# Seven block products in place of eight for a third of the tokens, with weight sums on GpSimd

## The chip, the cores and the metric

The kernel runs on one core of a Trainium2 chip. The metric is the device time of one execution in microseconds (us); the median of three runs is compared. Inputs and outputs lie in the chip's HBM. In the profile PE is TensorE's matmuls, PEld its weight loads, DVE is VectorE, ACT is ScalarE, POOL is GpSimd and SP is SyncE, whose queue issues most of the transfers.

## The reference

An attention block with a decay per head is followed by a mixer over tokens and channels.

```python
# q, k, v: (4, 8, 768, 64); blocks of 64 tokens, decay lam per head
intra = (q_b k_b^T * Dmask) v_b ;  inter = (q_b * lam_pow) kv_state
out_b = intra + inter ;  kv_state = lam**64 * kv_state + (k_b * rev_pow)^T v_b
x = out as (4, 768, 512)
xt = x.transpose(0, 2, 1)
h = xt @ U @ V                                   # U (768, 32), V (32, 768)
u = x + h.transpose(0, 2, 1)
ch = np.maximum(u @ w_ch1, 0.0) @ w_ch2          # (512, 2048), (2048, 512)
return (u + ch).astype(np.float32)
```

U, V, w_ch1 and w_ch2 come as float64, so each weight is read as two 32-bit words per element and converted on the chip. The two products with w_ch1 and w_ch2, over 3072 tokens, are the largest part of the work.

## The kernel before, in words

The 3072 tokens are six groups `g` of `N` = 512. The 2048 hidden columns are 16 tiles `ft` of 128. To keep float32 accuracy with TensorE's faster float32 type, each operand is split into a high part, a low part and a third part that mixes the two. A product of two blocks is then three matmuls, two adding to a bank `pz` and one to a bank `pd`; the value is `4097 * pz + 4096 * pd` with the scales used here.

The stages are, in the order of time:

- *Attention and mixer* (to about 114 us): an order written out by hand (`pieces`). Its output `u` is stored (`store`, `u_d`), turned by TensorE (`turn`) and split (`L609`, `L610`, `L613`, or `L640`, `L641`, `L633`) into `uhl` and `ud`, which stay in SBUF for all six groups.
- *First product* (114 to about 383 us): `hidden(ft, pair)` does one unit, a tile `ft` for a pair of groups: 16 matmuls to `pz` (L837), then 8 to `pd` (L848). ScalarE reads `pz` out (L844), VectorE adds `pd` (L853), and the result goes to HBM as `r_d[ft][g]` (L854). The first six units (`head`) are ordered by hand among the last pieces of the mixer. Then 33 units run tile by tile (`body`, `ft` 2 to 12) and 9 pair by pair (`tail`, `ft` 13 to 15). From the body on, a scheduler sets each engine's order. `banks` gives two sets of PSUM banks in turn.
- Beside these units `run_units` hands out the steps that make the weights. `weight_steps` fetches the float64 words (L146) and builds float32 from them: shifts and masks on VectorE (L166, L155), two exponent steps on ScalarE (L173, L174), three more steps on VectorE (L184, L192, L197). `split_steps` splits the result (L215, L220, L227, for w2 also L224). A tile of w1 goes into `w1_pool` (3 buffers) for `hidden`; a split tile of w2 goes to HBM (`w2_d`, 768 KB each) and comes back later (`w2_back`).
- *Second product* (to the end): 96 steps (`steps`, six groups by 16 tiles). `fetch` brings `r_d` back, `split` makes relu and the three parts (L952 on ScalarE; L953 and L954 on VectorE), `product` does 12 matmuls of 512 columns (L969, L971, L973). `ahead` runs the fetch three steps and the split two steps ahead. After 16 steps `finish` reads out four tiles (L990, L994) and adds `u` on GpSimd (L998).

Of the kernel before, what the change touches and what calls it, by code (L numbers as in the profile page):

```python
# [14 lines left out]
P = 128  # L15
# [3 lines left out]
def kernel(  # L19
# [61 lines left out]
    mix_ctx = ctx.enter_context(ExitStack())  # L81
    att_ctx = ctx.enter_context(ExitStack())
# [19 lines left out]
    w2_d = [dram.tile([P, 3, C], FP32, name=f"w2_d{ft}") for ft in range(FT)]  # L102
# [100 lines left out]
    def split_steps(tile_of, src, in_parts=False, scale=None, apart=False):  # L203

        st = {}

        def dst():
            if "w" not in st:
                st["w"] = wconv.tile([P, C], FP32, tag="wf", name="wf")
            return st["w"]  # L210

        def five():
            st["o"] = o = tile_of()
            st["t"] = o[:, 0, :].bitcast(FP32)
            on_scalar(lambda: nc.scalar.mul(o[:, 0, :], st["w"], NEAR))  # L215

        def six():
            w, low = st["w"], st["o"][:, 1, :]
            st["low"] = low.bitcast(FP32) if scale is None else w
            nc.vector.tensor_tensor(  # L220
                out=low if scale is None else w, in0=w, in1=st["t"], op=ALU.subtract
            )
            if scale is not None:
                on_scalar(lambda: nc.scalar.mul(low, w, scale))  # L224

        def seven():
            nc.vector.scalar_tensor_tensor(  # L227
                st["o"][:, 2, :], st["t"], -E, st["low"], ALU.mult, ALU.add
            )

        return weight_steps(dst, src, C, in_parts=in_parts, apart=apart) + [five, six, seven]

    w1v, w2v = {}, {}

    def w1_steps(ft, in_parts=False, apart=False):
        def tile_of():
            w1v[ft] = w1_pool.tile([P, 3, C], F32R, tag="w1", name="w1")
            return w1v[ft]

        cols = moe_w_ch1[:, ft * P : (ft + 1) * P].rearrange("(c p) f -> p c f", p=P)  # L240
        return split_steps(tile_of, cols, in_parts, apart=apart)
# [340 lines left out]
    def columns(what, g, ct):  # L582
        return what[:, ct, :] if g >= FG else by_halves(what)[:, :, ct, :]

    def like(out, g):
        return out if g >= FG else out.rearrange("p (t i) -> p t i", i=D)

    hl_at, d_at = [hl_pool], [d_pool]
# [4 lines left out]
    def turn(s):  # L593

        g, n = divmod(s, TG)
        if n == 0:
            uhl[g] = hl_at[g >= FG].tile([P, 2, CT, N], F32R, tag="hl", name="u_hl")
            ud[g] = d_at[g >= FG].tile([P, CT, N], F32R, tag="d", name="u_d")
        if g >= FG:
            cols = slice(n * P, (n + 1) * P)  # L600
            hi, low, diff = uhl[g][:, 0, :, cols], uhl[g][:, 1, :, cols], ud[g][:, :, cols]
            pt = bank([P, CT, P], "put", "b1")
            for ct in range(CT):
# [5 lines left out]
            nc.scalar.mul(hi, pt, E * NEAR)  # L609
            nc.vector.scalar_tensor_tensor(  # L610
                low, hi.bitcast(FP32), -1.0 / E, pt, ALU.mult, ALU.add
            )
            nc.gpsimd.tensor_tensor(  # L613
                out=diff, in0=hi.bitcast(FP32), in1=low.bitcast(FP32), op=ALU.subtract
            )
# [188 lines left out]
    def enter_first_product(s):  # L804
# [3 lines left out]
        for pools, name in ((hl_at, "hl_b"), (d_at, "d_b")):  # L808
            pools.append(
                ctx.enter_context(tc.tile_pool(name=name, bufs=NG - FG, reuse_waits="tile"))  # L810
            )
# [11 lines left out]
    def hidden(ft, pair, before={}):  # L823
# [28 lines left out]
        for g in pair:  # L852
            nc.vector.scalar_tensor_tensor(rs[g], acc[g][1], 4096.0, rs[g], ALU.mult, ALU.add)  # L853
            nc.sync.dma_start(out=r_d[ft][g], in_=rs[g])  # L854
# [218 lines left out]
```

## Time and profile before

| what | value |
|---|---|
| runs | 648.42, 649.17, 649.84 us; median 649.17 us |
| span of the profiled execution, first to last instruction | 648.1 us |
| PE busy | 639.3 us, 99% of the span |
| PEld, DVE, ACT, POOL busy | 539.3, 434.7, 268.8, 116.3 us |
| granted TensorE clock | 1.00 |
| moved by DMA | 131.69 MB, mean 203 GB/s |

The profiled execution's own time is not recorded apart from its span; the span is 0.3 us under the fastest run and 1.1 us under the median. Matmuls are pipelined, so their mean in the profile (389 to 391 ns for 512 columns) is longer than the time from one to the next. Durations of POOL are rough.

### The profile page before, as it was taken

The numbers are of one execution on the slowest core, as the hardware profiler recorded it, in microseconds if no ns is written. First come the engines' busy times: TensorE is split into PE (matmuls) and PEld (weight loads), VectorE is DVE, ScalarE is ACT, GpSimd is POOL, SyncE is SP. The second block draws the span as 40 slices with busy tenths as digits, with TensorE's granted clock in tenths as the row PEclk, the third lists the DMA queues.
The fourth block names the chain that finished last, engine by engine and source line by source line (L and its number), as shares of the span: only waits on it lengthen the run. The fifth ranks groups of instructions, "written<-read, shape, count | busy, mean of one in ns | idle before, by whom it ended". The sixth has DMA issues, their size and how long they took to land.

```text
span 648.1 us, 13405 instructions
## 1 busy us (share of the span) xinstructions
PE 639.3 (99%) x5242; PEld 539.3 (83%) x5242; DVE 434.7 (67%) x709; ACT 268.8 (41%) x500; POOL 116.3 (18%) x104
## 2 busy tenths in 40 slices
PE   9899999999999999999999999999999999999997
PEld 8888989788888888888888888888888888888886
DVE  6656878668997777777796244685575665755854
ACT  3675766435755444444454222332322322322320
POOL 4475968330000000000000000030030300300300
PEclk9999999999999999999999999999999999999999
DMA  9979996354876555655587899864363363543521
GB/s 232 241 182 272 231 242 163 119 191 176 287 258 219 209 207 209 207 209 211 211 292 276 320 332 392 287 220 138 96 227 98 123 204 97 172 152 99 179 82 65
DMA packets 132737, 131.69 MB, mean 203 GB/s; under 512 B 81538, under 2 KB 90754, under 8 KB 132674
## 3 DMA queue, kind: packets, MB, share of 16 engines
q1 hardware_dynamic: 107552, 124.41, 59.1%
q10 hardware_dynamic: 25122, 6.42, 4.4%
q8 instruction: 41, 0.67, 0.4%
q14 instruction: 22, 0.18, 0.1%
HBM read 80.09 MB, written 50.33 MB: 201 GB/s over the span
## 4 chain that ended last, share of the span: by engine, by line
PE 97%; ACT 1%; issue 1%; DMA 1%; DVE 0%; ACTq 0%; DVEq 0%
PE pz L837 27%; PE pd L848 13%; PE pz L971 13%; PE pz L969 13%; PE pd L973 13%; PE px L459 4%; PE pss L408 4%; PE px L470 2%; PE pqk L361 2%; PE pkv L431 1%; PE pm L563 1%; PE pp L486 1%; PE pm L626 1%; DMA kraw<-in_k_dram 1%; PE put L604 1%
## 5 line engine op out<-in xcount | busy, mean ns | idle before, releaser
L837 PE MATMUL pz<-u_hl,w 128*128 128x512 f32 x768 | 185.0, 391 | 0.0
L837 PEld LDWEIGHTS pz<-u_hl,w 128*128 128x128 f32 x768 | 143.7, 188 | 30.2 <-ACT r L844 0.6
L971 PE MATMUL pz<-w_hl,m 128*128 128x512 f32 x384 | 148.7, 389 | 0.0
L969 PE MATMUL pz<-w_hl,m 128*128 128x512 f32 x384 | 148.3, 389 | 0.0
L973 PE MATMUL pd<-w_d,m 128*128 128x512 f32 x384 | 147.4, 389 | 0.0
L952 ACT ACTIVATE m<-rm 128x512 fp32r<-128x512 f32 x96 | 60.6, 632 | 182.3 <-PE pd L973 125.5
L953 DVE SCALAR_TENSOR_TENSOR m<-rm,m 128x512 fp32r<-128x512 f32 x96 | 71.6, 748 | 95.7 <-ACT m L952 95.7
L998 POOL TENSOR_TENSOR o<-o,u 128x512 f32<-128x512 f32 x20 | 29.8, 1523 | 433.1 <-DVE o L994 433.1
L853 DVE SCALAR_TENSOR_TENSOR r<-pd,r 128x512 f32<-128x512 f32 x96 | 61.7, 685 | 60.4 <-ACT r L844 48.2
L848 PE MATMUL pd<-u_d,w 128*128 128x512 f32 x384 | 95.7, 390 | 0.0
L971 PEld LDWEIGHTS pz<-w_hl,m 128*128 128x128 f32 x384 | 72.1, 188 | 15.0
L969 PEld LDWEIGHTS pz<-w_hl,m 128*128 128x128 f32 x384 | 72.1, 188 | 15.0
L973 PEld LDWEIGHTS pd<-w_d,m 128*128 128x128 f32 x384 | 72.1, 188 | 14.7
L848 PEld LDWEIGHTS pd<-u_d,w 128*128 128x128 f32 x384 | 72.0, 188 | 14.9
L844 ACT ACTIVATE r<-pz 128x512 f32<-128x512 f32 x96 | 51.7, 591 | 66.9 <-PE pz L837 66.9
L954 DVE SCALAR_TENSOR_TENSOR m<-m 128x512 fp32r<-128x512 f32 x96 | 74.7, 779 | 3.0
L417 DVE TENSOR_TENSOR sm<-pss,mask 128x512 f32<-128x512 f32 x48 | 30.9, 686 | 18.0 <-PE pss L408 17.8
L215 ACT ACTIVATE w<-wf 128x512 fp32r<-128x512 f32 x32 | 20.3, 633 | 36.5 <-DVE wf L197 28.7
L173 ACT ACTIVATE sc<-sc,ends 128x512 f32<-128x512 uint32 x30 | 21.6, 721 | 22.8 <-DVE sc L166 22.8
L459 PE MATMUL px<-vraw,sm 128*64 128x64 f32 x768 | 29.0, 228 | 1.6 <-issue 1.4
L408 PE MATMUL pss<-qt,kt 64*128 64x128 f32 x384 | 29.0, 290 | 0.6 <-issue 0.5
L459 PEld LDWEIGHTS px<-vraw,sm 128*64 128x64 f32 x768 | 25.9, 140 | 3.4 <-issue 2.5
(91 smaller groups left out, 606.6 us busy)
## 6 DMA issues: line engine op xcount, KB each, us to landing
r_d<-r SPq DMA_DIRECT2D x96, 256.0 KB, 2.5
rm<-r_d SPq DMA_DIRECT2D x96, 256.0 KB, 2.7
words<-in_moe_w_ch_dram SPq DMA_DIRECT2D x30, 512.0 KB, 4.2
w_d<-w SPq DMA_DIRECT2D x16, 768.0 KB, 3.4
w_hl<-w_d SPq DMA_DIRECT2D x16, 512.0 KB, 6.2
u_d<-x_nat SPq DMA_DIRECT2D x24, 256.0 KB, 4.4
u<-u_d SPq DMA_DIRECT2D x24, 256.0 KB, 4.5
qraw<-in_q_dram SPq DMA_DIRECT2D x23, 256.0 KB, 4.8
```

Of the source, the lines that this page charges most:

```text
L408: nc.tensor.matmul(out=pss[:, x, a, :], lhsT=kt[half[x], a, :], rhs=qt[half[x], a, :], start=True, stop=True,)
L459: nc.tensor.matmul(out=px[half[t], x, a, :], lhsT=sm[:, x, a, half[t]], rhs=vr[:, 2 * a + x, :], start=(a == 0), stop=(alone and a == HP - 1),
L837: nc.tensor.matmul(out=like(acc[g][0], g), lhsT=w[:, n, ct, :], rhs=columns(uhl[g][:, n], g, ct), start=(ct == 0 and n == 0), stop=(ct == ...
L844: nc.scalar.mul(rs[g], acc[g][0], 4096.0 + 1.0)
L848: nc.tensor.matmul(out=like(acc[g][1], g), lhsT=w[:, 2, ct, :], rhs=columns(ud[g], g, ct), start=(ct == 0), stop=(ct == CT - 1),)
L853: nc.vector.scalar_tensor_tensor(rs[g], acc[g][1], 4096.0, rs[g], ALU.mult, ALU.add)
L952: nc.scalar.activation(out=m[:, 0], in_=r, func=AF.Relu, scale=NEAR)
L953: nc.vector.scalar_tensor_tensor(m[:, 1], r, 0.0, hi, ALU.max, ALU.subtract)
L954: nc.vector.scalar_tensor_tensor(m[:, 2], hi, E, low, ALU.mult, ALU.subtract)
L969: nc.tensor.matmul(out=pz, lhsT=m[:, 0, cols], rhs=hl[:, 0], start=first, stop=False)
L971: nc.tensor.matmul(out=pz, lhsT=m[:, 1, cols], rhs=hl[:, 1], start=False, stop=end)
L973: nc.tensor.matmul(out=pd, lhsT=m[:, 2, cols], rhs=dd, start=first, stop=end)
```

## The change

The last two groups (`g` = 4 and 5, or `FG` and `FG + 1`) leave the pairs of the first product. Their turned `u` is only copied, as float32, into `whole`. The units are now for four groups: 4 in the head, 22 in the body, and in the tail three for a pair and six for one group each. After the tail a second pass computes the first product of the two last groups. It takes the two groups, the two halves of the 512 channels and two neighbouring tiles `f`, `f2` of w1 as 2 x 2 blocks and forms seven block products in place of eight by Strassen's scheme (Winograd's order of sums): seven sums of blocks of `u`, split into three parts once (`form`), and seven sums of blocks of w1 for each pair of tiles.

The sums of w1 are made by GpSimd beside the body (`form_steps`), kept in HBM as float32 (`forms_d`), fetched in the second pass, two to a tile, and split then (`divided_steps`: ScalarE, VectorE, GpSimd). The plain tiles 0 and 1 of w1 are recomputed from their parts (`again`). Four chained products add to the same banks and are read out after each (`take`).

Further edits: the low part of a w1 tile is taken by GpSimd for `ft` > 1 (it was L220 on VectorE), and the `pd` of an odd group for `ft` > 1 is read by ScalarE and added by GpSimd. w2 is kept in HBM unsplit (256 KB each) and split when it comes back, four tiles during the second pass and twelve at the start of the second product.

```diff
-    w2_d = [dram.tile([P, 3, C], FP32, name=f"w2_d{ft}") for ft in range(FT)]
+    w2_d = [dram.tile([P, C], FP32, name=f"w2_d{ft}") for ft in range(FT)]
+    forms_d = [dram.tile([P, 7, C // 2], FP32, name=f"forms_d{j}") for j in range(FT // 2)]
...
+            (nc.gpsimd if ft > 1 else nc.vector).tensor_tensor(
+                out=w1v[ft][:, 1, :], in0=w1_plain[ft], in1=st["t"], op=ALU.subtract
+            )
...
+    def divided_steps(hi, low, third, fetch):
...
+        def split():
+            nc.scalar.mul(hi, st["w"], E * NEAR)
+            nc.vector.scalar_tensor_tensor(
+                low, hi.bitcast(FP32), -1.0 / E, st["w"], ALU.mult, ALU.add
+            )
+
+        def rest():
+            nc.gpsimd.tensor_tensor(
+                out=third, in0=low.bitcast(FP32), in1=hi.bitcast(FP32), op=ALU.subtract
+            )
...
-            nc.scalar.mul(hi, pt, E * NEAR)
-            nc.vector.scalar_tensor_tensor(
-                low, hi.bitcast(FP32), -1.0 / E, pt, ALU.mult, ALU.add
-            )
-            nc.gpsimd.tensor_tensor(
-                out=diff, in0=hi.bitcast(FP32), in1=low.bitcast(FP32), op=ALU.subtract
-            )
+            nc.scalar.copy(whole[g][:, :, n * P : (n + 1) * P], pt)
...
-            nc.vector.scalar_tensor_tensor(rs[g], acc[g][1], 4096.0, rs[g], ALU.mult, ALU.add)
+            if ft > 1 and g % 2:
+                low = r_pool.tile([P, N], FP32, tag="r", name="r_low")
+                nc.scalar.mul(low, acc[g][1], 4096.0)
+                nc.gpsimd.tensor_tensor(out=rs[g], in0=rs[g], in1=low, op=ALU.add)
+            else:
+                nc.vector.scalar_tensor_tensor(
+                    rs[g], acc[g][1], 4096.0, rs[g], ALU.mult, ALU.add
+                )
...
-    pairs = [(g, g + 1) for g in range(0, NG, 2)]
+    pairs = [(g, g + 1) for g in range(0, FG, 2)]
...
-    tail = [(pair, ft) for pair in pairs for ft in range(LAST, FT)]
+    tail = [(gs, ft) for gs in (pairs[0], *((g,) for g in pairs[1])) for ft in range(LAST, FT)]
...
+    def again(ft):
+        def step():
+            w, of = plain(w1_plain, ft)(), w1v[ft].bitcast(FP32)
+            nc.gpsimd.tensor_tensor(out=w, in0=of[:, 0, :], in1=of[:, 1, :], op=ALU.add)
+        return step
+
+    def form_steps(j):
...
+                nc.gpsimd.tensor_tensor(out=at[out], in0=at[a], in1=at[b], op=ALU.subtract)
...
+        return [some(5, 4, 0), some(7, 5, 2), some(7, 0, 1), some(6, 1, 3), keep]
...
+    for j in range(FT // 2):
+        sequence += [(j, 1), (j, 5)] + [(j - 1, 4)] * (j > 0) + [(j, i) for i in (6, 2, 3, 7)]
+    sequence.append((FT // 2 - 1, 4))
...
+    def form(p, n, i, of, engine=nc.vector):
...
+        nc.scalar.mul(hi, of, NEAR)
+        engine.tensor_tensor(out=low, in0=of, in1=hi.bitcast(FP32), op=ALU.subtract)
+        nc.vector.scalar_tensor_tensor(
+            d, hi.bitcast(FP32), E, low.bitcast(FP32), ALU.mult, ALU.subtract
+        )
...
+    run_units(tail[:3], side)
+    run_units(tail[3:6], early)
+    run_units(tail[6:8], late_forms + stream_steps[:6])
+    run_units(tail[8:], stream_steps[6:9])
...
+    def take(bank_pair, onto=None):
+        pz, pd = bank_pair
+        if onto is None:
+            t = r_pool.tile([P, N], FP32, tag="r", name="r")
+            nc.scalar.mul(t, pz, 4096.0 + 1.0)
+        else:
+            t = onto
+            nc.vector.scalar_tensor_tensor(t, pz, 4096.0 + 1.0, t, ALU.mult, ALU.add)
+        nc.vector.scalar_tensor_tensor(t, pd, 4096.0, t, ALU.mult, ALU.add)
+        return t
...
+    def one_of_seven(n):
+        j, p = sequence[n]
...
+        chain = {1: "c", 6: "c", 7: "c", 4: "c", 5: "b", 3: "b", 2: "a"}[p]
+        first = p in (1, 5, 2)
+        if first:
+            chains[j, chain] = banks(1, chain != "c")[0]
...
+                nc.tensor.matmul(
+                    out=pz, lhsT=w[:, i, rows], rhs=hl[:, i, c],
+                    start=first and c == 0 and i == 0, stop=c == 1 and i == 1,
+                    skip_group_check=True,
+                )
...
+        if p == 3:
+            u = kept.pop((j, 6))
+            nc.gpsimd.tensor_tensor(out=u, in0=u, in1=kept.pop((j, 3)), op=ALU.add)
+            give(u, f2, g0)
...
+    for n in range(len(sequence)):
+        one_of_seven(n)
+        for step in stream_steps[:2 if n % 2 else 1]:
+            step()
+        del stream_steps[:2 if n % 2 else 1]
+        if n >= 20 and n % 3 == 0 and w2_side:
+            w2_side.pop(0)()
...
-        if backs:
-            w2_back(backs.pop(0))
+        if i + 4 < FT:
+            for step in w2_split(i + 4):
+                step()
```

## The prediction

> **What bounds the kernel now.** I read the page first, then the chain of work that ended last, then the groups of instructions, and then single stretches of the timeline.
>
> ```profile
> span 648.1 us, 13405 instructions
> PE 639.3 (99%) x5242; PEld 539.3 (83%) x5242; DVE 434.7 (67%) x709; ACT 268.8 (41%) x500; POOL 116.3 (18%) x104
> ...
> PE 97%; ACT 1%; issue 1%; DMA 1%; DVE 0%; ACTq 0%; DVEq 0%
> ```
>
> TensorE (PE) is the chain: 97% of it. POOL is busy for 116.3 us, and the page's row of slices shows it empty from about 145 to 420 us, the stretch that this change rewrites. How fast one matmul follows another is read from the chain in order of time, where the profiled mean of 391 ns (a pipelined duration) would mislead:
>
> ```profile
> 160.00 3.63 PE pz L837 x16
> 163.63 1.81 PE pd L848 x8
> 165.45 3.63 PE pz L837 x16
> ```
>
> One unit of 24 matmuls starts every 5.45 us, so a matmul costs 5.44/24 = 0.2267 us. The next answer is the table of stretches, cut to the first product between 160 and 310 us (columns: length, then busy time and count of PE, PEld, DVE, ACT, POOL, then clock, DMA share, GB/s):
>
> ```profile
> 160.00:310.00 150.00, 150.00 (x664) 124.28 (x663) 116.97 (x204) 74.98 (x128) 0.00 (x0) 1.00 0.64 226
> ```
>
> PE is full, VectorE (DVE) is at 78%, POOL does nothing, the granted clock is 1.00, DMA is not full. The last view is the timeline around the end of a group of the second product, one of the few places where POOL works beside DVE operations whose two inputs both lie in SBUF (L953, L954):
>
> ```profile
> 424.60 0.69 DVE L953 SCALAR_TENSOR_TENSOR m<-rm,m 128x512 fp32r<-128x512 f32 x1 [1.30 <-ACT m L952]
> 425.21 2.49 DVE L994 SCALAR_TENSOR_TENSOR o<-pd,o 128x512 f32<-128x512 f32 x4
> ...
> 425.97 5.94 POOL L998 TENSOR_TENSOR o<-o,u 128x512 f32<-128x512 f32 x4 [282.77 <-DVE o L994]
> ...
> 427.62 1.44 DVE L954 SCALAR_TENSOR_TENSOR m<-m 128x512 fp32r<-128x512 f32 x1
> 428.98 1.78 DVE L953 SCALAR_TENSOR_TENSOR m<-rm,m 128x512 fp32r<-128x512 f32 x1
> ...
> 430.80 1.67 DVE L954 SCALAR_TENSOR_TENSOR m<-m 128x512 fp32r<-128x512 f32 x1
> ...
> 432.39 0.68 DVE L953 SCALAR_TENSOR_TENSOR m<-rm,m 128x512 fp32r<-128x512 f32 x1
> ```
>
> L953 and L954 take 0.69 us alone and 1.44 to 1.78 us while POOL runs. L994, with one input in PSUM, keeps 0.62 us each. Three operations lost 4.89 - 2.07 = 2.82 us to the 4.2 us of POOL work left after 427.7: **0.67 us of DVE per us of POOL**, as long as DVE stands at such an operation. In the attention part it is the same:
>
> ```profile
> 86.74 1.81 DVE L197 SCALAR_TENSOR_TENSOR wf<-m,sc 128x512 f32<-128x512 f32 x1
> 86.74 1.26 POOL L633 TENSOR_TENSOR u_d<-u_hl 128x512 fp32r<-128x512 f32 x1
> ```
>
> I call DVE operations with two SBUF inputs, and the SBUF-only shifts and masks of the weight conversion (L155, L166: median 0.42 and up to 1.24 us), port operations. DVE is the cover that this kernel runs under, and the change puts POOL on top of it.
>
> **The sum, part by part.** It is made against the profiled execution's span of 648.1 us; the three times have their median at 649.17, 1.1 us above it for what lies around the span.
>
> 1. *Matmuls.* Eight pairs of weight tiles need 7 block products of 6 matmuls in place of 8: 336 for 384. Minus 48 x 0.2267 = **-10.9 us** on PE. The left operands keep 128x128 and the right ones 512 columns, so I keep the pace. Nothing else on PE changes, and the head of the first product now has 4 units in place of 6.
>
> 2. *Body (22 units of four groups, 22 x 5.44 = 119.7 us of PE; before, 33 units for six groups).* Weights must now be made in two thirds of the time: 13 of w1 and 13 of w2. Counting the operations in the built DVE queue and pricing each with its median before (0.42 or 0.43 for L155 and L166, 0.68 to 0.69 for the others), I get 105.6 us, 88% of the stretch: 153 port operations (90.6 us) and 22 evictions. POOL, idle before, gets 13 subtractions of w1, 22 sums for the odd groups, 2 recomputed weights, all 128x512 at 1.285 us (L613 and L633 medians), 32 differences of 256 columns at 0.74 (between L530's 0.486 for 128 and 1.285 for 512), and 3 sums of 1024 at some 2.3: 78 us. The price of POOL on DVE runs from 0.67 x 78 x 0.62 = 32 us (port operations' share of a stretch so lengthened) to 0.67 x 78 x 0.85 = 44 us (DVE nearly always at one). DVE then needs 138 to 150 us for 119.7 of PE. The odd groups' eviction goes by ScalarE and hides; the even group's stands in the DVE queue behind the conversions, and PE gets its banks back only from there, two units later; that slack is spent once. So the body grows by 18 to 30 us. I take the middle, **+24**. That the conversions also wait for ScalarE (L173, L174: 0.72 us each) is in neither end.
>
> 3. *The seven products (56 x 1.36 = 76.2 us of PE).* Each is read out before the next one of its chain adds to the same banks, two products later: 2.7 us of slack. DVE: 64 reads from PSUM x 0.682 = 43.6, and 41 port operations x 0.69 plus one of 1024 columns = 29.5 (24 weight tiles, 4 of w2, 8 relu splits that stand early in the queue, the rest at the end): 73.1 of 76.2 us with no POOL at all. POOL has 45 operations, 57.8 us. Port operations are 37% of DVE's time, so the price is 0.67 x 57.8 x 0.37 = 14 us, and the stage takes 87: +11. At the other end POOL's third part follows the DVE operation that feeds it, and two reads from PSUM come next on DVE, so it may collide with nothing: 0. **+7**, nearer the row. The weight stream's transfers (two of 128 KB per tile; the median for 256 KB is 2.7 us) are issued six products, 8.2 us, ahead; ScalarE and the SP queue have room (about 60%, and 11 issues x 0.32 us per 9.5 us).
>
> 4. *Late split of w2.* Twelve tiles are split where the second product starts: 12 x 0.69 us on DVE and 12 x 1.285 on POOL, in a queue with the relu splits of steps 4 to 7. These are 23 port operations in some four steps (10.9 us). They run late against PE by the two steps of lead and more. Between 0 (lead holds) and 8 us (12 x 1.285 x 0.67 = 10.3 us more DVE, less the slack that is left), **+4**. What it saves, 512 KB of each store and reload of w2 in a stretch where the DMA share was 0.96, hid behind PE: 0.
>
> 5. *The rest.* Eight splits less on DVE and POOL in the head, 1024-wide forms in the tail, 6 single-group units: DVE has some 27 us for 32.6 us of PE there. 0.
>
> Sum: 648.1 - 10.9 + 24 + 7 + 4 = 672.2, with 1.1 around it **673 us**. Ends: 656 (+18, 0, 0) and 690 (+30, +14, +8).
>
> On the collision the row above is the measure. The Trainium skill (SBUF — State Buffer, "Who interferes with whom") goes further: the engine that issues second fully blocks for the whole instruction of the other. The trace agrees that it blocks (1.78 for 0.69 us), though POOL work and port operations overlapped by a third. Taken whole, the rule would add POOL's 78 to the 90.6 us of port operations.
>
> **Rivals.** *PE stays the bound (faster).* If POOL mostly works where DVE reads PSUM or waits for other engines, its price stays under the 14 us that DVE has free in the body (119.7 - 105.6; that is 0.18 us per us of POOL, where the row says 0.67), and the stage of seven products fits its 76.2 us. Then 649.2 - 10.9 = 638.3 us. For it: DVE alone fits everywhere. Against it: both rows above, and a free share of only 12% in the body and 4% in the stage of products.
>
> *Only the chain of seven products stalls (same, or a little off).* Body hidden, stage and start cost 5 to 18 us: 643 to 656. For it: the stage has the least slack. Against it: the body collides more.
>
> *Full exclusion (much slower).* No overlap at all between POOL and port operations: the body takes 78 + 90.6 = 169 us (+49), the stage 57.8 + 29.5 = 87 (+11), the start +6: 704 us. The rule of the Trainium skill named above is this case. Against it: in the burst three operations and 4.2 us of POOL took 4.9 us, not 6.3.
>
> *The change does not do what it says.* The PE queue as built has 48 matmuls fewer, so this gets no chance of its own.
>
> **How the numbers follow.** Forecast (656 to 690): 0.61. PE bound (637 to 642): 0.24. Chain alone (643 to 656): 0.08. Full exclusion: 0.07. A range of 637 to 691 leaves out full exclusion and the outer parts of the forecast, under 2 in 10. Since cases of both signs count, the forecast's own range is 656 to 690. A measurement of this kernel tells some 0.2% (1.3 us). Below 647.9: PE bound and a quarter of the chain case, 0.26. Within: 0.03. Above: 0.71.
>
> **What would show it.** Right: in the body DVE is over 95% busy, the w1 and w2 conversions' means rise from 0.69 to 0.9 us and more, PE shows idle time released by DVE's or ScalarE's eviction, and a pair unit takes 6.2 to 6.9 us in place of 5.44; the stage of products takes over 80 us. Wrong: units stay at 5.44 us and the port operations keep medians near 0.69 although POOL is 60% busy; or the stall is in the weight stream, with ScalarE waiting for transfers.

## The result, and the profile after

The changed kernel takes 715.75 us (median of four runs, 713.89 to 717.79), the kernel before in the same session 649.50 us (648.42 to 649.84). The ratio is 1.102, 95% interval 1.0996 to 1.1047: slower by 66 us. The profiled execution took 716.77 us.

The page of the changed kernel, the lines that answer to those shown of before, and two rows of its 40 slices (POOL in tenths busy, PEclk in tenths of the full clock):

```profile
span 714.7 us, 13823 instructions
PE 659.0 (92%) x5194; PEld 541.0 (76%) x5194; DVE 518.3 (73%) x715; ACT 303.3 (42%) x563; POOL 305.3 (43%) x238
...
POOL 4567882187254525427669876813003030120300
PEclk9999999999999889999799989999999999999999
...
PE 60%; DVE 16%; DMA 8%; issue 7%; ACT 4%; POOL 3%; SPq 0%; ACTq 0%; DVEq 0%; POOLq 0%
```

TensorE does 48 matmuls less and is busy 19.7 us longer. It is 60% of the chain that ended last, where it was 97%. POOL fills the stretch that was empty, and the clock row is no longer all nines.

Next the table of stretches: the body, the tail, the seven products, the first 34 us of the second product. Columns: stretch, length, busy time and count of PE, PEld, DVE, ACT, POOL, then clock, DMA share, GB/s.

```profile
143.62:305.30 161.68, 137.38 (x530) 106.65 (x528) 129.65 (x165) 74.19 (x128) 80.93 (x70) 0.91 0.62 213
305.30:343.77 38.47, 35.49 (x145) 28.38 (x144) 29.34 (x31) 20.32 (x34) 19.41 (x11) 0.94 0.57 193
343.77:446.30 102.53, 86.36 (x340) 66.27 (x339) 90.46 (x113) 49.69 (x91) 76.79 (x50) 0.92 0.63 201
446.30:480.00 33.70, 30.76 (x134) 24.52 (x133) 29.04 (x30) 10.60 (x19) 18.11 (x12) 1.00 0.49 151
```

The matmuls of the first three need 119.7, 32.6 and 76.9 us at the pace of before (76.2 for the seven products and 0.7 for three matmuls of the second product that stand among them). So the body lost 42.0 us, the tail 5.9, the seven products 25.6, and the rest of the second product, 268.4 us for 264.6, lost 3.8. With the 10.9 us saved this makes +66.4, and the spans differ by 66.6.

Each row splits in two. Length less PE's busy time is time in which TensorE stood: 24.3, 3.0 and 16.2 us. PE's busy time less the time that the same matmuls needed before is slower matmuls: 17.7, 2.9 and 9.5 us, at clocks of 0.91 to 0.94. **Of the 73 us lost in the three stretches 43 are waits and 30 slower matmuls.** The clock does not account for all of the 30. Its record shows ten spells at half clock in these stretches, 3.4 or 6.8 us each and 47.8 us in all, so at most 24 us. The rest has another cause, since evict_and_low_on_dve, below, has 5 us of it in body and tail at a clock of 1.00; which one is not shown.

One place in the body shows both. The timeline of the engines around 221 to 237 us (start, length, engine, line; in brackets the idle time before, and what ended it):

```profile
221.20 1.87 POOL L958 TENSOR_TENSOR t<-wf 128x256 f32<-128x256 f32 x2 [4.53 <-DVE wf L199]
223.03 2.00 POOL L958 TENSOR_TENSOR t<-wf,t 128x256 f32<-128x256 f32 x2
225.00 1.29 POOL L227 TENSOR_TENSOR w<-wf,w 128x512 fp32r<-128x512 f32 x1
...
226.32 1.73 DVE L232 SCALAR_TENSOR_TENSOR w<-w 128x512 fp32r<-128x512 f32 x1 [2.10 <-POOL w L227]
227.97 0.68 DVE L194 SCALAR_TENSOR_TENSOR sc<-words,sc 128x512 uint32<-128x512 uint32 x1
...
229.41 0.43 DVE L168 TENSOR_SCALAR sc<-words 128x512 uint32<-128x512 uint32 x1
...
229.88 0.72 ACT L175 ACTIVATE sc<-sc,ends 128x512 f32<-128x512 uint32 x1 [6.37 <-DVE sc L168]
230.50 1.06 ACT L873 ACTIVATE r<-pz 128x512 f32<-128x512 f32 x2
...
231.13 6.35 PE L866 MATMUL pz<-u_hl,w 128*128 128x512 f32 x16 [4.75 <-ACT r L873]
...
239.16 3.79 PE L866 MATMUL pz<-u_hl,w 128*128 128x512 f32 x16
```

POOL makes four weight differences (L958), then the low part (L227). VectorE's third part (L232) waits for that, and takes 1.73 us while POOL is at its next addition. The next weight's shift (L168) is behind L232, ScalarE's exponent step (L175) waits for the shift, and the eviction (L873), which frees TensorE's bank and whose input was long there, is behind L175. TensorE waits 4.75 us, and then its 16 matmuls take 6.35 us in place of 3.79; the granted clock is 0.50 from 229.46 to 236.28 us.

The groups of instructions show the slowed conversions (busy us, mean ns, idle before them). In the kernel before, these means were 725, 684 and 708 ns:

```profile
L199 DVE SCALAR_TENSOR_TENSOR wf<-m,sc 128x512 f32<-128x512 f32 x32 | 35.8, 1119 | 1.1
...
L186 DVE SCALAR_TENSOR_TENSOR m<-words,m 128x512 f32<-128x512 uint32 (+2 forms) x34 | 30.9, 910 | 1.1
...
L232 DVE SCALAR_TENSOR_TENSOR w<-w 128x512 fp32r<-128x512 f32 x16 | 18.1, 1134 | 16.6 <-POOL w L227 16.6
```

The stage of seven products is lost mostly at its start. The timeline of DVE and PE there:

```profile
344.71 3.95 DVE L1026 TENSOR_TENSOR s_hl<-u_whole,s_hl 128x1024 fp32r<-128x1024 f32 x2
348.58 2.35 DVE L1027 SCALAR_TENSOR_TENSOR s_d<-s_hl 128x1024 fp32r<-128x1024 f32 x2
350.85 1.28 DVE L258 SCALAR_TENSOR_TENSOR w<-w,wf 128x512 fp32r<-128x512 f32 x2
352.06 2.28 DVE L1026 TENSOR_TENSOR s_hl<-u_whole,s_hl 128x1024 fp32r<-128x1024 f32 x1
354.26 0.68 DVE L1145 SCALAR_TENSOR_TENSOR r<-pd,r 128x512 f32<-128x512 f32 x1
...
354.99 1.22 PE L1174 MATMUL pd<-s_d,w 128*128 128x512 f32 x2 [6.07 <-DVE r L1145]
356.01 1.91 PE L1167 MATMUL pz<-s_hl,w 128*128 128x512 f32 x4
```

The first eviction (L1145) stands behind 9.9 us of token forms and splits, and TensorE waits 6.07 us. The four matmuls of L1167 then take 1.91 us (1.07 to 1.09 later in the stage).

### The profile page after: what moved, and what is told of

Its sections match the earlier page's. It is cut to its first block, busy times and chain, and to the rows that moved or that the text cites. A ratio compares the mean times of both kernels' runs of the same rounds, so it can differ in the third digit from the quotient of the medians.

```text
span 714.7 us, 13823 instructions
## 1 busy us (share of the span) xinstructions
PE 659.0 (92%) x5194; PEld 541.0 (76%) x5194; DVE 518.3 (73%) x715; ACT 303.3 (42%) x563; POOL 305.3 (43%) x238
## 4 chain that ended last, share of the span: by engine, by line
PE 60%; DVE 16%; DMA 8%; issue 7%; ACT 4%; POOL 3%; SPq 0%; ACTq 0%; DVEq 0%; POOLq 0%
PE pd L1098 11%; PE pz L1096 11%; PE pz L1094 11%; DMA words<-in_moe_w_ch_dram 4%; PE pz L866 4%; PE pz L1167 4%; PE px L491 3%; PE pss L440 3%; DVE wf L199 3%; PE pd L1174 2%; DVE sc L194 2%; PE px L502 2%; DVE r L1145 2%; POOL t L958 2%; PE pd L877 2%
## 5 line engine op out<-in xcount | busy, mean ns | idle before, releaser
L866 PE MATMUL pz<-u_hl,w 128*128 128x512 f32 x512 | 141.4, 426 | 21.6 <-ACT r L873 21.1
L866 PEld LDWEIGHTS pz<-u_hl,w 128*128 128x128 f32 x512 | 104.2, 207 | 51.6 <-ACT r L873 28.5
L1098 PE MATMUL pd<-w_d,m 128*128 128x512 f32 x288 | 111.1, 390 | 2.1 <-DVE m L1080 2.1
L1096 PE MATMUL pz<-w_hl,m 128*128 128x512 f32 x288 | 112.2, 390 | 0.0
L1094 PE MATMUL pz<-w_hl,m 128*128 128x512 f32 x288 | 112.2, 390 | 0.0
L885 POOL TENSOR_TENSOR r<-r,r_low 128x512 f32<-128x512 f32 x28 | 42.0, 1502 | 68.5 <-ACT r_low L884 68.5
L1167 PE MATMUL pz<-s_hl,w 128*128 128x512 f32 x224 | 64.4, 412 | 4.0 <-ACT r L1141 4.0
L1094 PEld LDWEIGHTS pz<-w_hl,m 128*128 128x128 f32 x288 | 54.1, 188 | 11.2
L1096 PEld LDWEIGHTS pz<-w_hl,m 128*128 128x128 f32 x288 | 54.1, 188 | 11.2
L1167 PEld LDWEIGHTS pz<-s_hl,w 128*128 128x128 f32 x224 | 44.7, 201 | 15.1 <-ACT r L1141 5.1
L263 POOL TENSOR_TENSOR w<-w 128x512 fp32r<-128x512 f32 x32 | 47.2, 1486 | 16.8 <-DVE w L258 15.4
L175 ACT ACTIVATE sc<-sc,ends 128x512 f32<-128x512 uint32 x30 | 21.6, 720 | 69.6 <-DVE sc L168 69.6
L1174 PE MATMUL pd<-s_d,w 128*128 128x512 f32 x112 | 37.8, 420 | 12.2 <-DVE r L1145 12.0
L449 DVE TENSOR_TENSOR sm<-pss,mask 128x512 f32<-128x512 f32 x48 | 30.9, 685 | 20.3 <-PE pss L440 20.3
L1145 DVE SCALAR_TENSOR_TENSOR r<-pd,r 128x512 f32<-128x512 f32 x56 | 37.7, 682 | 7.3 <-ACT r L1141 6.7
```

The lines of the kernel that those rows point to most:

```text
L263: nc.gpsimd.tensor_tensor(out=third, in0=low.bitcast(FP32), in1=hi.bitcast(FP32), op=ALU.subtract)
L866: nc.tensor.matmul(out=like(acc[g][0]), lhsT=w[:, n, ct, :], rhs=columns(uhl[g][:, n], ct), start=(ct == 0 and n == 0), stop=(ct == CT - 1 ...
L1094: nc.tensor.matmul(out=pz, lhsT=m[:, 0, cols], rhs=hi, start=first, stop=False)
L1096: nc.tensor.matmul(out=pz, lhsT=m[:, 1, cols], rhs=low, start=False, stop=end)
L1098: nc.tensor.matmul(out=pd, lhsT=m[:, 2, cols], rhs=third, start=first, stop=end)
L1145: nc.vector.scalar_tensor_tensor(t, pd, 4096.0, t, ALU.mult, ALU.add)
```

## The experiments

The theory: GpSimd's work in SBUF slows VectorE's operations there ("the port"); VectorE, late, makes TensorE wait; and a wait lowers the clock. The rivals: the queues, in which others wait for GpSimd's results; VectorE's own added work; the transfers. The table has the stages of every run whose weights go the way of the changed kernel, cut at the first matmul of the body and the first and last of the seven products: the start of the body, body and tail (152.3 by the pace of before), seven products (76.9), and the rest. The times are medians; the stages are those of the profiled execution, which for three_on_dve, at 684.58 us, was the longest of four.

| kernel | time, us | body starts at | body and tail | seven products | rest |
|---|---|---|---|---|---|
| changed kernel | 715.75 | 143.6 | 200.2 | 102.5 | 268.4 |
| low_on_dve | 704.75 | 144.3 | 186.9 | 100.6 | 269.1 |
| evict_on_dve | 690.77 | 143.2 | 176.1 | 100.6 | 268.5 |
| evict_and_low_on_dve | 679.68 | 144.3 | 163.4 | 101.6 | 268.5 |
| three_on_dve | 678.78 | 148.3 | 162.8 | 103.0 | 268.4 |
| stream_first | 681.44 | 146.4 | 166.6 | 97.2 | 269.2 |
| no_form_sums | 693.51 | 144.4 | 175.2 | 103.1 | 268.3 |
| no_stream_thirds | 708.35 | 148.0 | 197.6 | 93.5 | 268.4 |
| more_words | 709.93 | 142.8 | 194.7 | 101.9 | 268.3 |
| stores_by_pool | 710.14 | 144.1 | 196.9 | 99.9 | 268.7 |
| no_pool | 660.12 | 147.8 | 151.9 | 90.3 | 268.6 |
| no_pool_stream_first | 654.88 | 146.3 | 151.9 | 86.1 | 268.4 |
| evict_on_dve_pool_beside | 717.05 | 147.1 | 201.7 | 102.0 | 268.6 |
| evict_on_dve_beside_pinned | 712.44 | 144.5 | 193.8 | 101.3 | 268.6 |
| both_on_dve_beside_pinned | 698.68 | 144.6 | 181.1 | 100.4 | 268.5 |

The kernel before ran beside them in 649.7 to 651.7 us (medians), so up to 2 us between two rows can be the session's. The body starts anywhere from 142.8 to 148.3 us, in the kernel before at 143.5. No edit here was aimed at what stands ahead of it, and why these executions differ there stays open.

**pool_beside: GpSimd alone, on the kernel before.** Nothing else of the change is in it.

```diff
 # hidden(), each unit from the body on
+for x in range(3):
+    beside = scratch.tile([P, N], FP32, tag="s", name="beside")
+    some = w1v[ft][:, 2, :].bitcast(FP32)
+    nc.gpsimd.tensor_tensor(out=beside, in0=some, in1=some, op=ALU.add)
```

> The kernel before, with three additions of 128x512 per unit of the body and tail put on GpSimd beside it (117 in all; they read the third part of a w1 tile and write to a scratch tile that nothing reads). Nobody waits for them, so they can act only through what GpSimd and VectorE share. Collision theory: VectorE's operations with two SBUF inputs (L184, L192, L197, L220, L227) go from a mean of 0.69 us to 1.0 us and more while GpSimd is busy, VectorE rises from 78% to 95% and more of the stretch 160 to 310 us, and the time grows by 5 to 40 us. Queue theory (the loss of the changed kernel comes from engines that wait for one another in fixed orders, GpSimd among them): no wait is added, 649 to 651 us.

689.63 us (688.83 to 690.43), ratio 1.060 (1.0555 to 1.0654). Its stretch from 160 to 310 us, then groups of it:

```profile
160.00:310.00 150.00, 130.16 (x524) 98.94 (x523) 147.53 (x164) 59.93 (x103) 106.64 (x82) 0.98 0.51 176
```

```profile
L184 DVE SCALAR_TENSOR_TENSOR m<-words,m 128x512 f32<-128x512 uint32 (+2 forms) x34 | 34.3, 1010 | 0.6
...
L166 DVE TENSOR_SCALAR sc<-words 128x512 uint32<-128x512 uint32 (+2 forms) x34 | 30.9, 908 | 0.9
...
L853 DVE SCALAR_TENSOR_TENSOR r<-pd,r 128x512 f32<-128x512 f32 x96 | 61.6, 683 | 21.8 <-PE pd L848 13.1 <-ACT r L844 6.9 <-DMA words<-in_moe_w_ch_dram 1.7
```

Additions that nobody waits for, on the row that carried the prediction, take DVE from 78% to 98% and stop TensorE for 20 us there. L184 goes from 684 to 1010 ns, L166 from 459 to 908; L853, with one input in PSUM, stays at 683. Over the whole run DVE is 79.9 us longer busy (514.6 for 434.7) for 154.7 us more of POOL: **0.52 us per us**. The trace has no instruction that waited for these additions. The collision alone slows this kernel.

**pauses: the price of a wait.** Fifteen bursts of 24 matmuls are set into the kernel before, each but the first after a chain of steps on ScalarE. Other matmuls filled the first four chains, so ten pauses count.

```diff
+for count, steps_of in enumerate([0, 1, 2, 3, 4, 5, 6, 8, 10, 14, 0, 2, 4, 6, 1]):
+    hold = bank([P, N], "hold", "b1")
+    if count:
+        nc.tensor.matmul(out=hold, lhsT=z[:, 0:P], rhs=z, start=True, stop=True)
+    for i in range(24):
+        nc.tensor.matmul(out=hold, lhsT=w1v[1][:, i % 3, 0:P],
+                         rhs=uhl[0][:, i % 2, i % CT, :], start=i == 0, stop=i == 23)
+    nc.scalar.mul(z, hold, 1.0)
+    for i in range(steps_of):
+        nc.scalar.mul(z, z.bitcast(FP32), 1.0)
```

> The kernel before with a block behind the head of the first product: fifteen bursts of 24 matmuls (128x512), and between them PE waits for a chain of 1 to 15 copies on ScalarE (0.6 us each), so pauses of about 1 to 10 us. Its total time means nothing. Clock theory: behind a pause of over some 3 us the 24 matmuls take 7 to 9 us in place of 5.44, and behind a pause under 2 us they take 5.44. Rival, a pause costs its own length and no more: 5.44 us behind each pause.

803.71 us, one run; only its bursts count. Its timeline of PE (L921 ends the pause, L923 is the burst):

```profile
274.88 0.50 PE L921 MATMUL hold<-z 128*128 128x512 f32 x1 [0.75 <-ACT z L927]
275.22 5.62 PE L923 MATMUL hold<-u_hl,w 128*128 128x512 f32 x24
282.92 0.50 PE L921 MATMUL hold<-z 128*128 128x512 f32 x1 [2.07 <-ACT z L929]
283.25 7.26 PE L923 MATMUL hold<-u_hl,w 128*128 128x512 f32 x24
...
306.19 0.80 PE L921 MATMUL hold<-z 128*128 128x512 f32 x1 [4.72 <-ACT z L929]
306.79 7.83 PE L923 MATMUL hold<-u_hl,w 128*128 128x512 f32 x24
```

After 0.75 us of pause the burst keeps its 5.6 us. After 2.07 us it takes 7.26, after 4.72 us 7.60 and 7.83, after 7.37 us 8.15. Each of the nine pauses of 2.07 us and more cost 1.3 to 2.5 us again when it was over; after the 2.07 us the granted clock is 0.50 from 284.09 to 287.50 us. It is not a fixed price: in the changed kernel ten of the eleven waits of 1.59 us and more in the three stretches have a spell of half clock in or right behind them, and one of 2.48 us (to 373.57 us) has none. The Trainium skill (TensorE: Matmul & The Clock Gate, "Part 1: The HAM clock gate") puts the half clock after an idle window of some 3.4 us; the trace agrees that an idle TensorE comes back slow, but 2.07 us was enough here.

**evict_and_low_on_dve, low_on_dve, evict_on_dve: GpSimd's parts given back.** The first has both edits, the others one each.

```diff
 # w1_steps, the low part
-(nc.gpsimd if ft > 1 else nc.vector).tensor_tensor(
+nc.vector.tensor_tensor(
 # hidden, the eviction of the odd groups
-if ft > 1 and g % 2:
+if False:
```

> The changed kernel with two of its GpSimd parts undone: the low part of w1 and the eviction of the odd groups are on VectorE again; the weight sums, the third parts and the sums of the second pass stay on GpSimd. That takes 41 operations of 1.3 to 1.5 us from GpSimd and gives VectorE 41 of 0.69 us (28 us). Collision and queue theory (GpSimd's operations cost VectorE and the chains more than their own work): 690 to 708 us, body 161.7 us down to 135 to 152. Load theory (VectorE is simply over-full, at 80% of a lengthened body): VectorE's body load goes from 130 to 150 us and the time to 716 to 735 us.

> The changed kernel with one part undone: the low part of a first weight (the subtraction of L227, in the changed kernel 14 times 1.30 us on GpSimd) is again VectorE's; the eviction and the form differences stay on GpSimd. Undoing this and the eviction together took 36 us off. Theory of the queue: what costs is that VectorE's third part (L232) stands waiting for GpSimd's low part (16.6 us of waits), with the conversion's next shift behind it and ScalarE's eviction behind that; then this part alone gives most of the 36 us back: 681 to 694 us. Theory of the port: what costs is VectorE's wait while GpSimd is on the port, so each part costs by its time on GpSimd, 18 us of the 60 that both have: some 11 us of the 36, 701 to 709 us.

> The changed kernel with the eviction of every second group alone back on VectorE (28 additions on GpSimd of 1.5 us and as many passes of ScalarE fall away, 28 of 0.68 us come to VectorE); the low part stays on GpSimd, and so does VectorE's wait for it. Theory of the port: the part costs by its time on GpSimd, 42 us of the 60 that it has with the low part, which alone gave 11 us back; the two together gave 36: 688 to 694 us. Theory of the queue (each of the two waits is behind the other, so only both together free the chain): 698 us or more.

Both: 679.68 us (679.54 to 679.83), below both ranges. The low part alone: 704.75 (702.66 to 706.50). The eviction alone: 690.77 (690.27 to 693.23). Each of these two lies in the port's range. The parts give back 11.0 and 25.0 us, the two together 36.1, so they add up, each by its time on GpSimd (18.2 and 42.0 us: 0.6 us per us). VectorE got 28.7 us of work back (28 x 0.68 and 14 x 0.69) and the kernel is faster: the theory that VectorE's own load is what costs falls. So does the theory that its wait for the low part is: with the eviction given back that wait is still 16.6 us in all. Body and tail, the changed kernel first, then with both:

```profile
143.65:343.80 200.15, 172.88 (x674) 135.03 (x673) 159.02 (x195) 94.54 (x161) 100.33 (x81) 0.92 0.61 209
```

```profile
143.65:307.70 164.05, 157.63 (x674) 124.89 (x673) 152.15 (x228) 79.95 (x132) 48.24 (x40) 1.00 0.73 245
```

DVE is busy about as long, with work in place of collisions. What fell are TensorE's waits, 27.3 to 6.4 us, and its matmuls' own time, 172.9 to 157.6: 20.9 and 15.3 us, the whole 36. The 33 more instructions in its own queue hold VectorE up less than GpSimd did beside it.

**no_form_sums and more_words: the other candidates of the body.** The first leaves the 32 differences L958 out and stores plain blocks in their place; the second adds a buffer for raw words.

```diff
 # no_form_sums: some() makes nothing, keep() stores
-nc.sync.dma_start(out=forms_d[j][:, 3:7], in_=st["t"])
+for n, of in ((3, w1_plain[f]), (5, w1_plain[f2])):
+    nc.sync.dma_start(out=forms_d[j][:, n:n+2], in_=of.rearrange("p (c f) -> p c f", c=2))
 # more_words
+words_pool.append(
+    mid_ctx.enter_context(tc.tile_pool(name="words3", bufs=1, side="right", reuse_waits="tile")))
```

> The changed kernel without the 32 differences of w1 blocks on GpSimd; plain blocks are stored in their place, with as many transfers and bytes, so the second pass computes with other weights. It takes 30 us from GpSimd and nothing else. Collision theory: VectorE gets back 0.3 to 0.7 us for each us of GpSimd in the body, so 700 to 710 us. Queue theory: the low part of each w1 tile and the store of the sums no longer wait behind the differences (27 us of waiting on SP, 16.6 us of VectorE for L227): 690 to 705 us, and VectorE's waits for L227 fall below 5 us while its operations stay as long as they were.

> The changed kernel with a third buffer for the raw words of a weight, so that the transfer of the next weight (4.4 us in the chain of waits of the body, behind VectorE's last step of the conversion) starts one conversion earlier. If this coupling of transfers to VectorE sets the pace of the body: 706 us or less. If VectorE's slowed instructions and its wait for GpSimd set it: 713 to 718 us, as the changed kernel.

693.51 us (693.08 to 693.94): 22.2 us for 29 us of differences, 0.77 per us. This lies in the queue's range and outside the collision's. They stand together ahead of the low part, and VectorE's wait for it falls from 16.6 to 4.7 us, while VectorE is busy for only 5.1 us less (513.2 for 518.3) and L232 stays as long (1208 ns for 1134). So most of what the differences cost is waits, as the queue theory has it, and not longer operations. The third buffer: 709.93 us (707.68 to 713.72), 5.8 us, between the two expectations. The transfers' coupling has a share, a small one.

**evict_on_dve_pool_beside, evict_on_dve_beside_pinned, both_on_dve_beside_pinned: port or queue.** The eviction is VectorE's, and GpSimd makes an addition of the same size in its place, whose result nobody reads. In the first it adds a resident operand, in the others the result that VectorE has just made, so that it stands where the changed kernel had it; the last has the low part on VectorE too.

```diff
+if ft > 1 and g % 2:
+    some = uhl[g][:, 0, 0, :].bitcast(FP32)      # pinned: some = rs[g]
+    beside = scratch[0].tile([P, N], FP32, tag="s", name="beside")
+    nc.gpsimd.tensor_tensor(out=beside, in0=some, in1=some, op=ALU.add)
```

> The eviction of the odd groups on VectorE (690.8 us alone), and in the place of each of the 28 additions that GpSimd lost one of the same size there, which adds a resident operand to itself into scratch; nobody waits for it. GpSimd's time and its reads are as in the changed kernel, its place in the chains is not. Theory of the port alone: GpSimd's time is what costs, wherever its result goes; then the 25 us that undoing the eviction gave come back for the most part: 708 to 720 us. Theory of the queues: what the eviction costs is that its result is waited for (the store in SyncE's queue, with the fetch of the next words behind it, and ScalarE's second pass), and busy GpSimd costs little beside it: 690 to 698 us. In between, the two share it by what is found.

> As the one before with 28 free additions on GpSimd, but each now adds a result to itself that VectorE's eviction has just made, so that it stands where the changed kernel had its own addition; there they had all run between 146 and 202 us, with the low parts behind them (VectorE's wait for low parts rose from 16.6 to 34.0 us). The eviction is on VectorE, the low part on GpSimd (690.8 us without the additions). Theory of the port: GpSimd's 35 to 42 us cost wherever they stand: 708 to 718 us. Theory of the queue: GpSimd's time costs where a low part stands behind it; spread out, little: 691 to 698 us.

> The eviction and the low part on VectorE (679.7 us), and the same 28 additions spread beside them. No step of the conversion and no eviction waits for GpSimd now; what is left of its price is the port alone, 0.53 us of VectorE per us of GpSimd in the runs so far, some 18 to 22 us on a VectorE that is 93% busy in the stretch. Theory of the port: 692 to 708 us, and as much as in the run before this one. Theory of the queue: 679 to 687 us.

The first came out at 717.05 us (716.24 to 721.15) but does not tell them apart: the scheduler set the free additions in one row from 146 to 202 us, with low parts behind them:

```profile
145.86 17.90 POOL L893 TENSOR_TENSOR beside<-u_hl 128x512 f32<-128x512 f32 x16 [4.29 <-DMA u_d<-x_nat]
```

Pinned, they took 712.44 us (709.98 to 714.47), 21.7 over the eviction alone and so most of the 25.0 that the eviction had given, without ScalarE's second pass; with the low part on VectorE too, so that nothing in the conversion or the evictions waits for GpSimd, 698.68 us (696.35 to 703.62), 19.0 over 679.68. The last kernel, body and tail, then groups of POOL:

```profile
143.65:325.70 182.05, 165.86 (x677) 126.62 (x675) 171.20 (x230) 80.79 (x133) 81.46 (x65) 0.98 0.68 223
```

```profile
L893 POOL TENSOR_TENSOR beside<-r 128x512 f32<-128x512 f32 x28 | 43.2, 1544 | 89.6 <-DVE r L887 84.8 <-PE pd L877 4.8
```

43.2 us of additions make DVE 19.4 us longer busy over the run (536.9 for 517.5; 0.45 per us) and the kernel 19.0 us longer. With or without a part that waits for GpSimd the price is about the same: for these additions it is the port. A queue behind GpSimd matters where its work stands in a row ahead of what others need, as the weight differences do.

**stores_by_pool: SyncE's queue.** GpSimd issues the transfers that wait for its own results.

```diff
-nc.sync.dma_start(out=r_d[ft][g], in_=rs[g])
+(nc.gpsimd if ft > 1 and g % 2 else nc.sync).dma_start(out=r_d[ft][g], in_=rs[g])
-nc.sync.dma_start(out=forms_d[j][:, 3:7], in_=st["t"])
+nc.gpsimd.dma_start(out=forms_d[j][:, 3:7], in_=st["t"])
```

> The changed kernel, in which GpSimd itself issues the transfers that wait for its results: the stores of the odd groups' sums (L890) and of the weight differences (L967). In SyncE's queue these waited 20.1 and 27.0 us in the body, with the fetches of words behind them. Theory of SyncE's queue: the fetches come earlier, VectorE waits less for words (9.6 us) and PE less for ScalarE: 700 us or less. Theory that the port and VectorE's own order set the pace: 710 to 720 us, and above that if issuing costs GpSimd time.

710.14 us (706.47 to 711.34). VectorE's wait for words falls from 9.6 to 1.2 us, and the kernel is 5.6 us faster, in the range of the second theory. But the issues themselves keep GpSimd busy for 20.3 us, and VectorE is busy for 11.6 us longer (529.9 for 518.3), so what the freed queue alone would give is not shown.

**no_stream_thirds, three_on_dve, stream_first: the seven products.** The first leaves out the 28 third parts of the weight forms and lets the matmuls read the low part. The second gives the token forms (L1026, L1032) to VectorE, on top of eviction and low part. The third has these two back and changes the order at the seam.

```diff
 # no_stream_thirds: rest() returns at once for the stream, and
-out=pd, lhsT=w[:, 2, rows]
+out=pd, lhsT=w[:, 1, rows]
 # three_on_dve: form(1, ...) and form(2, ...) by nc.vector, and in sums()
-nc.gpsimd.tensor_tensor(out=out, in0=a, in1=b, op=op)
+nc.vector.tensor_tensor(out=out, in0=a, in1=b, op=op)
 # stream_first
-run_units(tail[3:6], early)
-run_units(tail[6:8], late_forms + stream_steps[:6])
+run_units(tail[3:6], early + stream_steps[:3])
+run_units(tail[6:8], stream_steps[3:6] + late_forms[:1])
 ...
 form(7, 3, 0, a21)
+late_forms[1]()
```

> The changed kernel without the 28 third parts of the weight forms of the seven products (L263 on GpSimd, some 1.6 us each, 45 us); the third product reads the low part in their place, so the matmuls, transfers and VectorE's work stay. The stage takes 102.5 us in the changed kernel, where its matmuls alone need 76.2. Theory of the steady stream: VectorE's splits and evictions are slowed by these subtractions for the whole stage (its busy time 90.5 us where the rows of the kernel before give 73), so the stage becomes 84 to 92 us and the kernel 702 to 707 us. Theory of the start: the stage is lost at its start and at single stalls with the slower clock behind them, where VectorE stands in 1024-wide forms; then the stage stays over 96 us and the kernel at 710 us or more.

> The eviction and the low part back on VectorE (679.7 us alone), and with them the six 1024-wide operations of the token forms (the sums of L1032 and the two subtractions of L1026 that GpSimd made, 16 us there): on VectorE some 1.2 us each, 7.3 us. Theory of the start: the waits of 5.0 and 2.9 us and the slow clock behind them, at the start of the seven products, come from forms that collide with GpSimd's; without that the kernel takes 665 to 674 us. Theory that VectorE has no room there for more work: 679 to 687 us.

> The kernel with the eviction and the low part back on VectorE (679.7 us), and with another order at the seam: the splits of the first weight forms (L258) are issued a unit earlier and the token forms that are needed third and later behind them. The stage of the seven products took 101.6 us there, with waits of 5.0 and 2.9 us at its start for evictions and splits that stood behind 1024-wide forms in VectorE's queue, and a slow clock after them. Theory of the order: these 8 us and some 3 to 5 us of slow matmuls go: 667 to 674 us. Theory that VectorE is full there, so that a wait in another place takes their place: 677 to 683 us.

Without the third parts the stage takes 93.5 us, 9.0 less, between the two expectations; the wait of 6 us at its start stays. With the token forms on VectorE: 678.78 us (677.54 to 684.58), no gain. With the other order 681.44 us (681.15 to 681.99), no gain: the stage is 4.4 us shorter, body and tail 3.2 longer (and the body starts 2.2 later). VectorE is full at that seam, busy for 31.9 of the 32 us from 313 us on, and what is set ahead there is late elsewhere. The theory of the start's order falls for kernels with GpSimd at work.

**no_pool, no_pool_stream_first: what is left without GpSimd.** Eviction, low parts and token forms on VectorE; differences and third parts left out as above; the second also with the order of stream_first.

> As the one with the eviction, the low part and the token forms on VectorE, and without the differences of the weight forms (plain blocks are stored in their place, the same transfers) and without the 28 third parts of the seven products: GpSimd then has next to nothing beside the conversions and the seven products; the matmuls and VectorE's own work are complete. If GpSimd on the port and in the queues is all of the loss beyond VectorE's own sum, the body and the tail come out by VectorE's uncontended rows: 105.6 of the conversions, 29 of the eviction and low parts, some 32 of the tail with its forms, 166 us where the matmuls need 152, the seven products at 76 to 80, the second product 4 longer: 650 to 662 us. If VectorE's added work hides wholly: 640 to 648. If transfers and waits of the second pass itself cost, without GpSimd: 670 us or more.

> The same order in the kernel whose GpSimd was relieved throughout (eviction, low parts and token forms on VectorE; differences of the weight forms and the 28 third parts left out; 660.1 us). Its stage of the seven products took 90.3 us, with a wait of 5.4 us for a split at its start. By the order: 649 to 655 us, so that even without GpSimd's work the saving of 10.9 us is used up by the late w2 split, the start of the stage and what VectorE's added work leaves visible. If VectorE is full: 657 to 663 us.

660.12 us (656.94 to 662.74) and 654.88 us (654.42 to 657.05), ratio 1.0071 (1.0049 to 1.0094) for the second. Each lies in its first range, the first of them by luck: it had 166 us for body and tail and 76 to 80 for the seven products, which took 151.9 and 90.3. The body and tail of the first, then the seven products of the second:

```profile
143.65:299.70 156.05, 156.05 (x691) 129.14 (x691) 140.91 (x239) 84.64 (x139) 1.29 (x1) 1.00 0.82 267
```

```profile
298.20:384.30 86.10, 80.73 (x340) 62.43 (x339) 83.50 (x116) 48.41 (x85) 31.49 (x22) 1.00 0.75 238
```

The first row begins 4.2 us ahead of the body. From its first matmul on, at 147.8 us, body and tail take 151.9 us, no more than their matmuls need. TensorE never stands there and the clock is 1.00, though VectorE, with the eviction, the low parts and the token forms on it, is busy for 90% of the row. So in body and tail VectorE's own work hides wholly once GpSimd is silent, and the whole loss there goes with GpSimd's work. The seven products still take 86.1 us, 9.2 over, with DVE busy for 83.5 of them. GpSimd still has 31.5 us of work there, so how much of the 9.2 is VectorE's own load is not shown. These 9.2 and the 3.8 of the late split use up the saving of 10.9. A further 2.8 us stand ahead of the body in this execution, which spans 652.7 us for 648.1; the medians differ by 4.3. No version that computes everything came near 650.

## Why the prediction was wrong, step by step

The direction and the collision were right; the step from VectorE's load to TensorE's time was not. 715.75 us lies 43 over the forecast and 26 above the range.

*Matmuls, -10.9: right.* The seven products run at 1.36 us each, start to start, wherever nothing stalls.

*The collision: right in kind, and its rate was right.* I took 0.67 x 0.62 to 0.67 x 0.85, 0.42 to 0.57 us of DVE per us of POOL; pool_beside gives 0.52, the pinned additions 0.54 and 0.45. POOL's load in the body came to 80.9 us for 78. The load that it was added to was too high. 13 and 13 conversions make 143 port operations, which with the 22 evictions are the 165 of the body's row, not the 153 of the sum. And between 160 and 310 us of before such operations sum to 126.3 us where DVE was busy for 117.0, as neighbours overlap. By both, 105.6 us should have been some 92 (an estimate), and 129.65 measured is 38 more, 0.47 per us of POOL.

*The body, +24, measured +42: the step that failed.* It set the body's length equal to VectorE's busy time, 138 to 150 us. VectorE was busy for 129.65 us only and idle for 32, in waits for POOL (16.6), for ScalarE (9.5) and for words (7.6). I had left ScalarE out of both ends, and did not follow who stands behind VectorE in order: shift, exponent step, eviction, bank. A pair unit took 7.35 us on average, where I had 6.2 to 6.9. That TensorE's waits came to 24.3 us, the number that I gave, is chance. The other 17.7 us are a term that the sum did not have, slower matmuls, most of them from the clock after a wait (0.91 over the body, at most 14 us). A stall was priced at its own length.

*The stage of products, +7, measured +25.6.* The steady collision was sized well: the third parts cost 9.0 us, within my 0 to 11 (the upper end of the whole sum used 14, VectorE's added time, for this stage). The sum took the stage to begin with empty queues. But from 329 to 340 us, in the tail, 1024-wide forms on DVE (3.2 and 3.4 us each) ran beside POOL's own 1024-wide forms and sum, and the stage began with 9.9 us of forms and splits still queued on DVE and a wait of 6.07 us. That belongs to step 5: *the rest at 0* failed, by 5.9 us in the tail and by the backlog handed on. And 73.1 of 76.2 us of DVE was taken as fitting; with more than half of POOL's work gone such a load still cost 9.2 us. Of the 25.6 us 16.2 are waits and 9.5 slower matmuls, at most 8 of them by the clock.

*The late split of w2, +4: right*, 3.8 us.

*The rivals.* "PE stays the bound" fell in both trace and experiment. Full exclusion gave 704, the nearest number, by the wrong way: it wanted POOL and port operations end to end, 169 us in the body, where VectorE was busy for 130 while POOL was for 81. The rule behind it (the Trainium skill, SBUF — State Buffer, "Who interferes with whom": the second to issue is blocked for the other's whole instruction) fits single rows, L232 at 1.73 us for 0.69, but per us of POOL the runs show 0.45 to 0.54 us, not one.

*What would show it.* Means of 0.9 us and more (L194 alone stayed under it, at 0.78), idle time released by evictions, and a stage above 80 us were there. "DVE over 95% busy" was not: 80% in the body. That line already says that the length of such a stretch isn't its fullest engine's busy time.

## What to carry to other kernels

An idle engine is free room only if its operations do not slow the others'. In this kernel each microsecond of GpSimd beside VectorE's conversions cost about half a microsecond of VectorE. Add that before work goes to GpSimd, and take the sum as a lower bound of the stretch: it made some 130 us of VectorE in the body here, and the body took 161.7. How full VectorE is does not tell by itself. At 80% of the body TensorE stood for 24.3 us; at 90% without GpSimd it did not stand at all.

Price a stall of TensorE of 2 us and more at its length plus 1.3 to 2.5 us of slow matmuls; here that mostly held. And where a stage is sized, price its first ten microseconds apart, with what the stage before leaves in the queues.

## What the runs showed of the hardware

- A pause of 0.75 us left the pace alone, one of 2.07 us cost 1.6 us afterwards. In the changed kernel the granted clock is half for ten spells of 3.4 or 6.8 us in the three stretches, at most 24 of the 73 us lost there, and 0.966 on average over the whole run.
- VectorE's shifts and masks within SBUF, with one tensor input, collide too: 459 to 908 ns (L166) beside GpSimd.
- GpSimd pays as well: its 128x512 operation had a median of 1.285 us in the kernel before (L633), and took 1.50 (L885 of the changed kernel) and 1.54 us (L893 of both_on_dve_beside_pinned) on average beside a busy VectorE.
- VectorE busy for 90% of body and tail (no_pool, 140.9 of 156.1 us) did not stop TensorE once while GpSimd was silent.
